# A fused attention and two-layer MLP kernel: two sums of each pair stay in PSUM, and token work, values and first-pair steps are given other places in the order

## The chip, the cores and the metric

The kernel runs on one core of one Trainium2 chip. The metric is the device time of one execution in microseconds, as the median of several runs. The profile shows one execution: TensorE (PE for matmuls, PEld for weight loads), VectorE (DVE), ScalarE (ACT), GpSimd (POOL) and SyncE (SP, which issues the DMAs).

## The reference

Forgetting attention on 4 batches of 8 heads, 576 positions, 64 values a head, then a gated MLP and a second MLP on the 2304 tokens of width 512, all fp32:

```python
cum = np.cumsum(np.maximum(s, 0.0), axis=-1)
bias = -(cum[:, :, :, None] - cum[:, :, None, :])
scores = np.where(causal, -1e9, scale * q @ k.T + np.minimum(bias, 0.0))
attn = softmax(scores)
x = (attn @ v) laid out as [2304, 512]
# first MLP: w_gate, w_val [512, 1536], w_out [1536, 512]
g = x @ w_gate
x = (g * sigmoid(g) * (x @ w_val)) @ w_out
# second MLP: w_in [512, 2048], w_out [2048, 512]
h = x @ w_in
out = (h * sigmoid(h)) @ w_out
```

## The kernel before, in words

Every fp32 product is made of three matmuls on a high and a low part (`mm3`, L448 to L450): high by high, high by low, low by high. Cutting a tile into the two parts is a copy on ScalarE (`copy`, L100) and a subtraction, mostly on GpSimd (L426, L460, L518).

The first layer is a row of 36 chunks of weights, nine for each batch (`L1`: six "gv" chunks for the gate and value matrices, three "o1" chunks for the way down). The attention of batch 0 stands ahead of them. Chunks 0 to 26 run in a loop (`for c in range(last)` in `body`) in which the MLP of batch b is interleaved with the attention of batch b + 1: the table `at` says after which quarter of a chunk the scores, the transposes (L271, L277) and the values (`value`, L312, bank `pv`) of a head pair are issued. In this loop only TensorE's order is that of the code; a scheduler sets the order of the other engines. The weights come packed as 64-bit numbers, and in batch 0 each chunk also unpacks the weights of the next (`unpack`, L369 to L374: two ScalarE and two VectorE steps on each of four pieces; the intermediate `dk` lies in one of the four banks of the pool `ps_m`, which the gates, `pgv`, and the sums of the way down, `po`, use by turns). Unpacked pieces are stored to memory (`w_store`) for the later batches. The list `later` deals 32 pieces of the second layer's weights out over the chunks from batch 1 on; each is loaded a chunk ahead of its unpacking (`ahead_load`, `ahead`).

Chunks 27 to 35 are batch 3, without attention; all engines run in the order of the code. The results of layer 1 are stored to `x_d` (L490) as they are complete. The tokens of the first of three groups are loaded again (`x2_load`, L508), combined (`x2_sub`, L532) and cut (`x2_cut`, L518) for the second layer, in the steps of the lists `more` and `extra`.

The second layer has 24 steps, one for each of three token groups t and eight pairs p of weight columns. In each, `up2` forms four products of 2x2 blocks by seven products xi = 0 to 6 (a scheme like Strassen's and Winograd's) in four banks a, d, b, c of `ps_m`; copies of banks (`s0`, `s1`, `s4`, L621), sums with them (L626, L632, L636), a tanh (L591), the gate product (`gated`, L598) and the cut into `h` follow on the other engines. `down2` of the step before (L657 to L659) then adds into `acc` (L664, L666). Weights of the second layer are combined (`u_sum`), cut (`u_cut`) and, for the later groups, stored (`u_store`, to `wu_d`). The dictionary `fills` says behind which product of `up2` ("u", xi) or which part of `down2` ("d", n) such work is issued. The temporaries of these steps take the place in SBUF of tiles of the first layer.

Of the kernel before, what the change touches and what calls it, by code (L numbers as in the profile page):

```python
# [56 lines left out]
def kernel(  # L57
# [520 lines left out]

    def up2(i, fill):
        t, p = steps[i]  # L580
# [13 lines left out]
        def gated(k):  # L594
            src = u[k]
            if k == 0:
                u[k] = part("u0")
            nc.vector.scalar_tensor_tensor(out=u[k], in0=th[k], scalar=1.0, in1=src, op0=ALU.add, op1=ALU.mult)  # L598
# [6 lines left out]
        for name, k, xi, bank in UP:  # L605
# [22 lines left out]
            if xi == 4:  # L628
                nc.gpsimd.tensor_tensor(out=tmp["s1"], in0=tmp["s1"], in1=tmp["s4"], op=ALU.add)
                nc.gpsimd.tensor_tensor(out=tmp["s1"], in0=tmp["s1"], in1=tmp["u2"], op=ALU.add)  # L630
            if xi == 5:
                nc.vector.tensor_tensor(out=part("c12"), in0=o, in1=tmp["u2"], op=ALU.add)  # L632
                tanh(1, tmp["c12"])
                gated(1)
            if xi == 6:
                nc.vector.tensor_tensor(out=part("c21"), in0=o, in1=tmp["u2"], op=ALU.add)  # L636
                tanh(3, tmp["s1"])
                cut(1)
                gated(3)
                tanh(2, tmp["c21"])  # L640
                cut(3)
                gated(2)
                cut(2)
            for f in fill.get(("u", xi), []):
# [105 lines left out]
    def body():  # L750
# [33 lines left out]
        for i in range(NPR * CW // DW):  # L784
            later[len(L1) + i if i < 18 else 3 * len(L1) + (i - 18) // 2].append(i)
        p2["wt"], p2["st"] = wt_p, raw_p
        for c in range(last):
# [3 lines left out]
            if b + 1 < B:  # L791
                k, u0 = c % len(L1), (b + 1) * H
                if k < H:
                    if k > 1:
                        at[0].append(lambda x=u0 + k - 2: value(x))
                    at[0].append(lambda x=u0 + k: scores(x))
                    if k > 0:
                        at[2].append(lambda x=u0 + k - 1: transpose(x))
                else:
                    at[0] += [lambda x=u0 + k - 2: value(x), lambda x=u0 + k - 1: transpose(x)]  # L800
                    at[2].append(lambda x=u0 + k - 1: value(x))
            for n, stp in enumerate(cur):
# [21 lines left out]
        for c in range(last, n1):  # L824
# [14 lines left out]
            g = nc.gpsimd  # L839
            if k == 2:  # L840
                more[2].append(lambda: x2_load(0))
            if k == 3:
                extra = [
                    lambda: x2_sub(0, 1),
                    lambda: (x2_cut(0, 0, None, g), x2_sub(0, 2)),
                    lambda: x2_cut(0, 1, p2["t", 1], g),
                    lambda: x2_cut(0, 2, None, g),
                ]
            if k == 6:
                extra = [  # L850
                    lambda: (x2_cut(0, 3, p2["t", 2], g), x2_sub(0, 3)),
                    lambda: (x2_cut(0, 4, p2["t", 3], g), x2_sub(0, 4)),
                    lambda: x2_cut(0, 5, None, g),
                    lambda: x2_cut(0, 6, p2["t", 4], g),
                ]
            if k == 7:
# [8 lines left out]
            for n, stp in enumerate(cur):  # L865
                if n == 0:
                    wst.pop(c - 1, None)
                stp()
                todo = more[n] if len(cur) == 4 else more[n // 2] if n % 2 == 0 else extra[n // 2 : n // 2 + 1]
                late, stores = stores, []  # L870
                for f in todo:
                    f()
                if n % (len(cur) // 4) == 0:
                    e = n // (len(cur) // 4) - 2
                    if 0 <= e < len(later[c]):
                        stores.append(later[c][e])
                for i in late:
                    ahead_store(i)
        first_layer.close()
        p2["acc"] = pool("acc2", 1, scope=second_layer)  # L880
        p2["h"] = pool("h2", 8, scope=second_layer)
        p2["tmp"] = pool("tmp2", 1, scope=second_layer)
        p2["wt2"] = pool("wt2", 4, scope=second_layer)
        p2["st"] = pool("st", 4, scope=second_layer)
        fills = [{} for _ in range(len(steps) + 1)]

# [3 lines left out]
        g, v = nc.gpsimd, nc.vector  # L890
        put(0, ("u", 0), lambda: u_cut(0, "D", v), lambda: u_raw(1, "D"))
        put(0, ("u", 3), lambda: u_store(0))
        put(0, ("u", 5), lambda: u_raw(2, "Z"))
        put(0, ("u", 6), lambda: u_store(1, "ZS"))
# [17 lines left out]
        for t in range(1, TG):  # L912
# [3 lines left out]
            put(i - 1, ("d", 7), lambda t=t: x2_cut(t, 0, None, g))  # L916
            put(i, ("u", 0), lambda t=t: x2_cut(t, 1, p2["t", 1], g), lambda t=t: x2_sub(t, 2))
            put(i, ("u", 1), lambda t=t: (x2_sub(t, 3), x2_sub(t, 4)))
            put(i, ("d", 1), lambda t=t: x2_cut(t, 2, None, v))
# [6 lines left out]
        for i in range(len(steps)):  # L926
            up2(i, fills[i])
            if i > 0:
# [50 lines left out]
```

## Time and profile before

| | |
|---|---|
| median of 3 runs | 1092.18 us (1090.01 to 1092.25) |
| the profiled execution | 1095.51 us, its span 1093.7 us |
| TensorE busy | 1038.3 us (95%), 7008 matmuls |
| VectorE, ScalarE, GpSimd busy | 60%, 52%, 56% |
| mean granted clock of TensorE | 0.978 |

Busy time of TensorE near the whole span leaves some 55 us of idle time. Part of the idle time lies in the attention of batch 0, ahead of 97 us, which the change doesn't touch.

### The profile page before, as it was taken

To read this page: it belongs to the slowest core of one execution; us is meant where nothing else is said; L and a number is where in the kernel's file an instruction comes from. 1 tells how busy PE (TensorE), PEld (TensorE's weight loads), DVE (VectorE), ACT (ScalarE), POOL (GpSimd) and SP (SyncE) were. 2 spreads that over 40 slices of the span, in tenths; PEclk is the share of its full clock that TensorE was granted. 3 is DMA by queue.
4 is the path that set the end of the run, shared out by engine and by line. 5 is a ranking of instruction groups with operands and counts; after the bars stand their busy time and mean duration, and the time that the engine had idled before them with its cause. 6 is when DMAs were issued, how large, how long until landed. Compare 5 with 4: busy or idle time off the path is not lost.

```text
span 1093.7 us, 19585 instructions
## 1 busy us (share of the span) xinstructions
PE 1038.3 (95%) x7008; PEld 963.9 (88%) x7008; DVE 654.3 (60%) x1529; ACT 565.1 (52%) x1251; POOL 607.3 (56%) x702
## 2 busy tenths in 40 slices
PE   8779899989999999999999998799989999999998
PEld 5448889879989899898999998799989999999998
DVE  5668676835655546546534657667785454744554
ACT  6658776735665546666424554454443433443331
POOL 4555656554766557757435767466675343743342
PEclk8879999999999999999999999999999999999999
DMA  9556586563546375332335662858767664564521
GB/s 224 140 171 207 195 243 211 164 184 120 179 125 177 110 203 157 115 132 93 122 111 192 238 191 103 301 218 286 278 259 238 231 252 162 181 245 164 183 77 58
DMA packets 70481, 197.96 MB, mean 181 GB/s; under 512 B 9008, under 2 KB 28464, under 8 KB 64240
## 3 DMA queue, kind: packets, MB, share of 16 engines
q1 hardware_dynamic: 70384, 196.72, 55.1%
q8 instruction: 55, 0.90, 0.4%
q14 instruction: 42, 0.34, 0.1%
HBM read 146.28 MB, written 50.41 MB: 180 GB/s over the span
## 4 chain that ended last, share of the span: by engine, by line
PE 72%; DVE 11%; DMA 5%; ACT 5%; issue 3%; POOL 2%; SPq 0%; DVEq 0%; ACTq 0%; POOLq 0%
PE pgv L448 7%; PE pgv L450 7%; PE pgv L449 7%; PE po L657 5%; PE po L659 5%; PE po L658 5%; PE pu L615 4%; PE pu L619 4%; PE pu L618 4%; PE pv L312 4%; PE po L448 4%; PE po L450 4%; PE po L449 4%; PE psc L201 4%; PE ptr L271 3%
## 5 line engine op out<-in xcount | busy, mean ns | idle before, releaser
L448 PE MATMUL pgv<-xt,wt 128*128 128x288 f32 x768 | 230.1, 300 | 6.9 <-DVE acc L488 3.5
L449 PE MATMUL pgv<-xt,wt 128*128 128x288 f32 x768 | 226.3, 295 | 0.0
L450 PE MATMUL pgv<-xt,wt 128*128 128x288 f32 x768 | 226.3, 295 | 0.0
L426 POOL TENSOR_TENSOR wt<-wraw,wt 128x1024 fp32r<-128x1024 f32 x72 | 172.2, 2404 | 94.3 <-ACT wt L100 92.1
L448 PEld LDWEIGHTS pgv<-xt,wt 128*128 128x128 f32 x768 | 144.3, 188 | 19.3 <-issue 7.0
L449 PEld LDWEIGHTS pgv<-xt,wt 128*128 128x128 f32 x768 | 144.3, 188 | 0.0
L450 PEld LDWEIGHTS pgv<-xt,wt 128*128 128x128 f32 x768 | 144.2, 188 | 0.0
L657 PE MATMUL po<-h,wt 128*128 128x384 f32 x384 | 131.7, 343 | 3.0 <-DVE acc L666 2.2
L460 POOL TENSOR_TENSOR h<-u,h 128x288 fp32r<-128x288 f32 x96 | 82.9, 867 | 89.3 <-ACT h L100 89.2
L659 PE MATMUL po<-h,wt 128*128 128x384 f32 x384 | 129.1, 336 | 0.0
L658 PE MATMUL po<-h,wt 128*128 128x384 f32 x384 | 129.0, 336 | 0.0
L615 PE MATMUL pu<-x,wt 128*128 128x384 f32 x336 | 114.8, 342 | 9.7 <-ACT s L621 9.7
L231 ACT ACTIVATE e<-e,m 64x64 f32<-64x64 f32 (+4 forms) x160 | 88.5, 554 | 60.0 <-DVE m L218 59.2
L448 PE MATMUL po<-h,wt 128*128 128x288 f32 x384 | 115.2, 300 | 0.8 <-DVE acc L488 0.6
L619 PE MATMUL pu<-x,wt 128*128 128x384 f32 x336 | 114.5, 341 | 0.0
L618 PE MATMUL pu<-x,wt 128*128 128x384 f32 x336 | 114.3, 340 | 0.0
L450 PE MATMUL po<-h,wt 128*128 128x288 f32 x384 | 113.3, 295 | 0.0
L449 PE MATMUL po<-h,wt 128*128 128x288 f32 x384 | 113.1, 294 | 0.0
L100 ACT ACTIVATE h<-u 128x288 fp32r<-128x288 f32 (+1 forms) x120 | 54.8, 457 | 105.2 <-DVE u L458 82.5
L666 DVE SCALAR_TENSOR_TENSOR acc<-po,acc 128x384 f32<-128x384 f32 x168 | 86.5, 548 | 22.6 <-PE po L659 22.2
L457 DVE SCALAR_TENSOR_TENSOR u<-th,pgv 128x288 f32<-128x288 f32 x96 | 43.2, 450 | 93.9 <-ACT th L455 79.2
L621 ACT ACTIVATE s<-pu 128x384 f32<-128x384 f32 x72 | 35.2, 490 | 110.2 <-PE pu L619 110.2
(99 smaller groups left out, 2345.2 us busy)
## 6 DMA issues: line engine op xcount, KB each, us to landing
wt<-wu_d SPq DMA_DIRECT2D x32, 1024.0 KB, 6.2
wraw<-w SPq DMA_DIRECT2D x54, 512.0 KB, 4.7
r<-in_w_dram SPq DMA_DIRECT2D x52, 512.0 KB, 6.2
wu_d<-wt SPq DMA_DIRECT2D x16, 1024.0 KB, 6.3
wt<-wu_d SPq DMA_DIRECT2D x16, 768.0 KB, 4.6
qkr<-in_qk_dram SPq DMA_DIRECT2D x32, 288.0 KB, 6.9
w<-wraw SPq DMA_DIRECT2D x18, 512.0 KB, 4.2
cumb<-cum_d SPq DMA_DIRECT2D x15, 576.0 KB, 8.4
```

What stands on the lines that cost most here:

```text
L231: nc.scalar.activation(out=e[:r, hd, :wd], in_=e[:r, hd, :wd], func=AF.Exp, bias=m[hd][:r], scale=-1.0, accum_out=l[:r, hd : hd + 1],)
L426: engines[WL[phase[c]][e]].tensor_tensor(out=wl, in0=t, in1=wh.bitcast(F32), op=ALU.subtract)
L448: nc.tensor.matmul(out=ps[:, :n], lhsT=a, rhs=xh, start=(k == 0), stop=False)
L449: nc.tensor.matmul(out=ps[:, :n], lhsT=a, rhs=xl, start=False, stop=False)
L450: nc.tensor.matmul(out=ps[:, :n], lhsT=c, rhs=xh, start=False, stop=(k == last))
L615: nc.tensor.matmul(out=o, lhsT=a, rhs=x[:, 0, kk], start=fresh and kk == 0, stop=False, skip_group_check=True)
L618: nc.tensor.matmul(out=o, lhsT=a, rhs=x[:, 1, kk], stop=False, **more)
L619: nc.tensor.matmul(out=o, lhsT=c, rhs=x[:, 0, kk], stop=kk == 1, **more)
L657: nc.tensor.matmul(out=ps, lhsT=a, rhs=hi, start=f == 0, stop=False)
L658: nc.tensor.matmul(out=ps, lhsT=a, rhs=lo, start=False, stop=False)
L659: nc.tensor.matmul(out=ps, lhsT=c, rhs=hi, start=False, stop=f == 1)
L666: nc.vector.scalar_tensor_tensor(out=a, in0=ps, scalar=0.5, in1=a, op0=ALU.mult, op1=ALU.add)
```

## The change

In the second layer two of the sums of a pair are written back into their banks in place of SBUF, and their gate products read them there into tiles of their own (`w1`, `w2`); `gated(1)` is issued one product later. The closing steps of the first pair (`tail`) are issued behind products 0, 1 and 2 of the second pair. Two loads (`u_raw`) are issued ahead of the first pair. The pool of the temporaries is opened behind those of the weights, so that it lies elsewhere. At the end of a group one cut of tokens is issued in the way down. In batch 3 the load, the subtractions and the cuts of tokens are dealt out over chunks 0 to 6 of the batch; the list `later` starts a chunk later. In the loop over chunks, `value` moves from the start of a chunk to its first quarter, or from the half to three quarters.

```diff
         def gated(k):
             src = u[k]
-            if k == 0:
-                u[k] = part("u0")
+            if k != 3:
+                u[k] = part(f"w{k}")
             nc.vector.scalar_tensor_tensor(out=u[k], in0=th[k], scalar=1.0, in1=src, op0=ALU.add, op1=ALU.mult)
...
             if xi == 4:
-                nc.gpsimd.tensor_tensor(out=tmp["s1"], in0=tmp["s1"], in1=tmp["s4"], op=ALU.add)
-                nc.gpsimd.tensor_tensor(out=tmp["s1"], in0=tmp["s1"], in1=tmp["u2"], op=ALU.add)
+                nc.gpsimd.tensor_tensor(out=part("w3"), in0=tmp["s1"], in1=tmp["s4"], op=ALU.add)
+                nc.gpsimd.tensor_tensor(out=tmp["w3"], in0=tmp["w3"], in1=tmp["u2"], op=ALU.add)
             if xi == 5:
-                nc.vector.tensor_tensor(out=part("c12"), in0=o, in1=tmp["u2"], op=ALU.add)
-                tanh(1, tmp["c12"])
+                nc.vector.tensor_tensor(out=o, in0=o, in1=tmp["u2"], op=ALU.add)
+                tanh(1, o)
+            if xi == 6:
                 gated(1)
-            if xi == 6:
-                nc.vector.tensor_tensor(out=part("c21"), in0=o, in1=tmp["u2"], op=ALU.add)
-                tanh(3, tmp["s1"])
-                cut(1)
-                gated(3)
-                tanh(2, tmp["c21"])
-                cut(3)
-                gated(2)
-                cut(2)
+                nc.vector.tensor_tensor(out=o, in0=o, in1=tmp["u2"], op=ALU.add)
+                tail = [
+                    lambda: (tanh(3, tmp["w3"]), cut(1)),
+                    lambda: (gated(3), tanh(2, o), cut(3), gated(2)),
+                    lambda: cut(2),
+                ]
+                for e, f in enumerate(tail):
+                    if i == 0:
+                        later_on.setdefault(("u", e), []).append(f)
+                    else:
+                        f()
...
-            later[len(L1) + i if i < 18 else 3 * len(L1) + (i - 18) // 2].append(i)
+            later[len(L1) + 1 + i if i < 17 else 3 * len(L1) + (i - 17) // 2].append(i)
...
                     if k > 1:
-                        at[0].append(lambda x=u0 + k - 2: value(x))
+                        at[1].append(lambda x=u0 + k - 2: value(x))
                     at[0].append(lambda x=u0 + k: scores(x))
...
-                    at[0] += [lambda x=u0 + k - 2: value(x), lambda x=u0 + k - 1: transpose(x)]
-                    at[2].append(lambda x=u0 + k - 1: value(x))
+                    at[1] += [lambda x=u0 + k - 2: value(x), lambda x=u0 + k - 1: transpose(x)]
+                    at[3].append(lambda x=u0 + k - 1: value(x))
...
-            if k == 2:
+            if k == 0:
                 more[2].append(lambda: x2_load(0))
-            if k == 3:
-                extra = [
-                    lambda: x2_sub(0, 1),
-                    lambda: (x2_cut(0, 0, None, g), x2_sub(0, 2)),
-                    lambda: x2_cut(0, 1, p2["t", 1], g),
-                    lambda: x2_cut(0, 2, None, g),
-                ]
-            if k == 6:
-                extra = [
-                    lambda: (x2_cut(0, 3, p2["t", 2], g), x2_sub(0, 3)),
-                    lambda: (x2_cut(0, 4, p2["t", 3], g), x2_sub(0, 4)),
-                    lambda: x2_cut(0, 5, None, g),
-                    lambda: x2_cut(0, 6, p2["t", 4], g),
-                ]
+            sub = {1: 1, 2: 2, 4: 3, 5: 4}.get(k)
+            cuts = {1: [0], 2: [1], 3: [2, 3], 4: [4], 5: [5], 6: [6]}.get(k, [])
+            if sub:
+                more[0].append(lambda: x2_sub(0, sub))
+            for e, x in enumerate(cuts):
+                src = None if x in (0, 2, 5) else {1: 1, 3: 2, 4: 3, 6: 4}[x]
+                f = lambda x=x, src=src: x2_cut(0, x, None if src is None else p2["t", src], g)
+                if len(cur) == 4:
+                    more[2].append(f)
+                else:
+                    extra.append(f)
...
-                todo = more[n] if len(cur) == 4 else more[n // 2] if n % 2 == 0 else extra[n // 2 : n // 2 + 1]
+                todo = more[n] if len(cur) == 4 else more[n // 2] if n % 2 == 0 else extra[n // 4 : n // 4 + n // 2 % 2]
...
-        p2["tmp"] = pool("tmp2", 1, scope=second_layer)
         p2["wt2"] = pool("wt2", 4, scope=second_layer)
         p2["st"] = pool("st", 4, scope=second_layer)
-        fills = [{} for _ in range(len(steps) + 1)]
+        p2["tmp"] = pool("tmp2", 1, scope=second_layer)
+        u_raw(1, "D")
+        u_raw(2, "Z")
+        fills, tails = [{} for _ in range(len(steps) + 1)], {}
...
-        put(0, ("u", 0), lambda: u_cut(0, "D", v), lambda: u_raw(1, "D"))
+        put(0, ("u", 0), lambda: u_cut(0, "D", v))
         put(0, ("u", 3), lambda: u_store(0))
-        put(0, ("u", 5), lambda: u_raw(2, "Z"))
...
-            put(i, ("u", 0), lambda t=t: x2_cut(t, 1, p2["t", 1], g), lambda t=t: x2_sub(t, 2))
-            put(i, ("u", 1), lambda t=t: (x2_sub(t, 3), x2_sub(t, 4)))
+            put(i, ("u", 0), lambda t=t: (x2_sub(t, 2), x2_sub(t, 3)))
+            put(i, ("u", 1), lambda t=t: x2_sub(t, 4))
+            put(i, ("d", 0), lambda t=t: x2_cut(t, 1, p2["t", 1], g))
...
-            up2(i, fills[i])
+            up2(i, fills[i], tails if i == 0 else None)
+            fills[i + 1] = {k: tails.pop(k, []) + fills[i + 1].get(k, []) for k in {*tails, *fills[i + 1]}}
```

At the start of chunk 2 TensorE's order before is this: the last gate matmul of chunk 1, the values of a head pair (`pv`), the scores of another (`psc`), the first gate matmul of chunk 2.

```order
L450 MATMUL pgv<-xt,wt 128x288
L312 MATMUL pv<-pt,vz 64x320 x2
L312 MATMUL pv<-pt,vrb 64x256 x2
L312 MATMUL pv<-pt,vrb 64x128 x2
L201 MATMUL psc<-qkr 128x64 x2
L201 MATMUL psc<-qkr 128x192 x2
L201 MATMUL psc<-qkr 128x320 x2
L448 MATMUL pgv<-xt,wt 128x288
```

With the change it is:

```order
L450 MATMUL pgv<-xt,wt 128x288
L201 MATMUL psc<-qkr 128x64 x2
L201 MATMUL psc<-qkr 128x192 x2
L201 MATMUL psc<-qkr 128x320 x2
L448 MATMUL pgv<-xt,wt 128x288
```

The rows of `pv` now stand behind the first gate step of the chunk; the first bank of `ps_m` in chunk 2 is that of a gate.

In chunk 8, the last of batch 0, ScalarE's order before has the unpacking of a second-layer piece (`dk<-r`) ahead of a tanh of the gates (`th<-pgv`); `pt<-ptr` copies transposed scores, `xt<-pv` values.

```order
L100 ACTIVATE pt<-ptr 128x2x384
L370 ACTIVATE dk<-r_3189 128x512
L455 ACTIVATE th<-pgv 128x288
L100 ACTIVATE h<-u 128x288
L455 ACTIVATE th<-pgv 128x288
L100 ACTIVATE wt<-wraw 128x1024 x2
L100 ACTIVATE h<-u 128x288
L100 ACTIVATE xt<-pv 128x320
L100 ACTIVATE pt<-ptr 128x1024
L100 ACTIVATE xt<-pv 128x256
```

With the change it is:

```order
L100 ACTIVATE pt<-ptr 128x2x384
L455 ACTIVATE th<-pgv 128x288
L100 ACTIVATE h<-u 128x288
L455 ACTIVATE th<-pgv 128x288
L100 ACTIVATE wt<-wraw 128x1024 x2
L100 ACTIVATE h<-u 128x288
L100 ACTIVATE xt<-pv 128x320
L100 ACTIVATE pt<-ptr 128x1024
L370 ACTIVATE dk<-r_3366 128x512
L100 ACTIVATE xt<-pv 128x256
```

`dk<-r` has moved behind every tanh of the chunk, with one copy of values behind it.

Between the first and the second pair of the second layer, ScalarE's order before is this, from the copy of product 4 of the first pair on (`s_9230` and `s_9244` are those of products 0 and 1 of the second pair; `c` are the two sums).

```order
L621 ACTIVATE s_9180<-pu 128x384
L591 ACTIVATE th<-c_9190 128x384
L591 ACTIVATE th<-s_9147 128x384
L100 ACTIVATE h_9123<-c_9190 128x384
L591 ACTIVATE th<-c_9203 128x384
L100 ACTIVATE h_9125<-s_9147 128x384
L100 ACTIVATE h_9124<-c_9203 128x384
L621 ACTIVATE s_9230<-pu 128x384
L621 ACTIVATE s_9244<-pu 128x384
L100 ACTIVATE wt<-stage 128x1024
```

With the change it is this (`s_9218` and `s_9236` are now those of the second pair):

```order
L621 ACTIVATE s_9182<-pu 128x384
L591 ACTIVATE th<-pu 128x384
L621 ACTIVATE s_9218<-pu 128x384
L591 ACTIVATE th<-w_9184 128x384
L100 ACTIVATE h_9127<-w_9202 128x384
L621 ACTIVATE s_9236<-pu 128x384
L591 ACTIVATE th<-pu 128x384
L100 ACTIVATE h_9129<-w_9184 128x384
L100 ACTIVATE wt<-stage 128x1024
L100 ACTIVATE wt<-stage 128x768
L591 ACTIVATE th<-pu 128x384
L100 ACTIVATE h_9128<-w_9243 128x384
```

The two copies of the second pair have moved ahead of most closing steps of the first, and a last cut of the first pair (`h_9128`) stands behind the first tanh of the second.

## Rows read from the trace of the kernel before

**Rows 1.** First line of the page.
```profile
span 1093.7 us, 19585 instructions
```

**Rows 2.** Waits of TensorE, 97.7 to 255.6 us: total, times, longest.
```profile
PE pv L312 <- DVE wraw L374: 5.4, 5, 3.1
PE pv L312 <- DVE u L457: 4.9, 1, 4.9
PE pgv L448 <- DVE wraw L374: 1.1, 1, 1.1
...
```

**Rows 3.** Waits of TensorE, 566.1 to 689.5 us (batch 3).
```profile
PE pgv L448 <- DVE acc L488: 3.5, 2, 2.5
PE pgv L448 <- DVE u L457: 2.4, 3, 1.6
PE po L448 <- DVE acc L488: 0.6, 1, 0.6
```

**Rows 4.** Waits of TensorE, 689.5 us to the end (second layer).
```profile
PE pu L615 <- ACT s L621: 9.7, 4, 3.9
PE po L657 <- DVE acc L666: 2.2, 7, 0.4
PE po L657 <- ACT acc L664: 0.9, 2, 0.4
```

**Rows 5.** Windows: busy us (instructions) of PE, PEld, DVE, ACT, POOL; PEclk; DMA.
```profile
236.05:239.46 3.41, 3.41 (x19) 2.40 (x16) 1.12 (x3) 3.17 (x6) 2.21 (x2) 0.50 0.00 0
239.46:242.87 3.41, 3.41 (x29) 3.41 (x28) 2.17 (x3) 1.15 (x2) 3.41 (x3) 1.00 0.37 120
710.50:713.91 3.41, 3.40 (x11) 3.40 (x12) 2.00 (x3) 1.00 (x3) 2.82 (x3) 0.50 0.97 394
713.91:717.32 3.41, 3.41 (x21) 3.41 (x20) 1.62 (x2) 2.70 (x8) 2.88 (x3) 1.00 0.48 194
...
812.90:816.31 3.41, 3.41 (x12) 3.41 (x11) 2.19 (x3) 1.18 (x4) 2.32 (x3) 0.50 0.00 0
```

**Rows 6.** Timeline of ScalarE, chunks 3 and 8: start, duration, [idle before, releaser].
```profile
149.30 1.23 ACT L369 ACTIVATE wraw<-r 128x512 f32<-128x512 f32 x2 [2.56 <-DMA w<-wraw]
...
234.18 0.66 ACT L370 ACTIVATE dk<-r 128x512 uint32<-128x512 uint32 x1 [9.24 <-DMA r<-in_w_dram]
```

**Rows 7.** Timeline of VectorE in batch 3.
```profile
619.26 2.33 DVE L371 SCALAR_TENSOR_TENSOR dk<-z,dk 128x512 uint32<-128x512 uint32 x1
...
623.78 0.68 DVE L371 SCALAR_TENSOR_TENSOR dk<-z,dk 128x512 uint32<-128x512 uint32 x1
```

**Rows 8.** Timeline of SyncE, TensorE and VectorE around the second pair.
```profile
691.30 2.99 SPq L575 DMA_DIRECT2D wu_d<-wt  x3
694.39 1.22 SPq L550 DMA_DIRECT2D stage<-w  x1
...
702.10 0.44 PE L615 MATMUL pu<-x,wt 128*128 128x384 f32 x1 [2.88 <-ACT s L621]
...
704.74 3.18 DVE L561 TENSOR_TENSOR stage<-stage 128x256 f32<-128x256 f32 x4 [3.63 <-DMA stage<-w]
```

**Rows 9.** Groups by line and form: count, busy us, mean ns, idle before.
```profile
L598 DVE SCALAR_TENSOR_TENSOR c<-th,c 128x384 f32<-128x384 f32 x48 | 49.6, 1034 | 20.7 <-ACT th L591 20.7
L598 DVE SCALAR_TENSOR_TENSOR s<-th,s 128x384 f32<-128x384 f32 x24 | 13.4, 558 | 6.4 <-ACT th L591 6.4
L598 DVE SCALAR_TENSOR_TENSOR u<-th,pu 128x384 f32<-128x384 f32 x24 | 13.3, 552 | 63.3 <-ACT th L591 63.3
```

**Rows 10.** Timeline of VectorE, GpSimd and TensorE at the first group's end.
```profile
806.62 0.94 DVE L532 TENSOR_TENSOR stage<-x2r,stage 128x768 f32<-128x768 f32 x1
807.19 2.07 POOL L518 TENSOR_TENSOR x<-stage,x 128x768 fp32r<-128x768 f32 x1 [1.77 <-ACT x L100]
807.49 2.59 DVE L532 TENSOR_TENSOR stage<-x2r 128x768 f32<-128x768 f32 x1
...
812.40 0.44 PE L615 MATMUL pu<-x,wt 128*128 128x384 f32 x1 [2.67 <-ACT s L621]
```

More of the change, by code (lines that the diff above doesn't have):

```diff
@@ L577, in u_store, with up2 @@
             )
-    def up2(i, fill):
+    def up2(i, fill, later_on):
         t, p = steps[i]
```

## The prediction, made before the changed kernel ran

> **What bounds the kernel now.** The first line of the page gives the span, 1093.7 us [rows 1]. I read the waits of TensorE next, stage by stage, because the kernel can only get shorter where TensorE stands idle or runs at the low clock; its other work is the same set of matmuls after the change. In the chunk loop of batch 0 three rows are 11.4 us of idle time [rows 2]; batch 3 has 6.5 us [rows 3]; the second layer 12.8 us [rows 4]. [...] Nearly all of it is TensorE waiting for a bank of PSUM that VectorE or ScalarE has still to empty, so the question at each place is what these engines do instead, and for what they wait.
>
> **Chunk loop of batch 0.** Two things happen. First, the values start a quarter chunk later, behind the scores and the first gate step. The five waits of 5.4 us in all [rows 2] are for banks that held `dk` in the unpacking of the next weights; the order shows that the bank is now wanted by the gate behind the scores, so the scores are the cover, about as long as what stood ahead before. But the order also shows score work of VectorE put between two `dk`, so `dk` is done later; and the unpacking is a chain through memory: ScalarE stood 2.56 us until a store of decoded weights had left its buffer [rows 6], and that store is no earlier now. Of the 6.5 us of the `wraw` rows I count 1.2 as won. From below, each of the six chunks 2 to 7 could lose 0.7 us (4 us in all, a quarter of the 2.56 us wait in each); from above all 6.5 are won. I take a value near the lower end because the chain's waits are the longest that these rows show.
>
> Second, chunk 8. There the 4.9 us wait comes from one ScalarE row: `dk<-r` stood 9.24 us for a load and held back the tanh behind it [rows 6]. After the change this row stands behind all four tanh of the chunk, and the load is one of the next chunk's, so nothing that TensorE needs is queued behind it but one copy of values. This wins 4.9 us and the clock behind it, 1.2 us [rows 5]. Chunk loop: 1.2 + 4.9 + 1.2 = **7.3 us** (6.1 - 4 = 2.1, to 6.1 + 6.5 = 12.6).
>
> **Batch 3.** The waits are for VectorE (the sums into `acc`, the gate products) [rows 3], in the two chunks where x2 work is bunched. While GpSimd cuts tokens, VectorE's `dk<-z` takes 2.33 us; the next one, alone, 0.68 us [rows 7]: 1.65 us more for each row. Bunched, two unpackings and two subtractions follow one another there, 6.6 us late; spread over six chunks, half as many, 3.3 us, and the four banks that TensorE fills by turns cover most of that. The new order adds a wait: the first load of x2 goes out only half a chunk ahead of its first subtraction, behind which the gate products of that chunk are queued. I take a microsecond or two there as covered by the banks too. I count 4.9 of 6.5 us as won: the second cut of chunk 3 stands at its end, so that chunk 4 has two of them on GpSimd beside two of weights, which leaves about 1 us, and the last piece in chunk 7 about 0.6. Bounds: 3.5, if each chunk with a cut keeps half a microsecond (six chunks, 3 us), and 6.5.
>
> [...]
>
> **First pair into second pair.** Two waits for `s`. The first, 2.88 us [rows 8], is `s` of the second pair in ScalarE's queue behind the closing steps of the first; the order shows that these now stand between the `s` of the second pair. The second, 3.9 us [rows 4], is a chain: the load of `stage` was issued at 694.39 behind three stores that took 2.99 us; VectorE waited 3.63 us for it, until 704.74, then took 3.18 us for the sum, and the products and copies stood behind [rows 8]. Both loads now go out ahead of these stores, so the data lands 3 us earlier or more: VectorE's wait falls to 0.6 us or nothing. What is late next is the half-chain of the first pair: its last product must be out of its bank before the second pair takes it for its product 4, and `s1`, `gated` and three tanh stand in one queue. I leave one wait of 2 us there, and 1.1 us for the first step down, whose cover shrinks. Of 2.9 + 3.9 and the clock of 1.6, 8.4 in all, 8.4 - 2.0 - 1.1 = **5.3 us** is won (3.4, if one wait of 3.4 us stays and the clock falls once; 8.4). The temporaries now lie where the last outputs of layer 1 lay and wait for their stores; the stores are issued well ahead of the first use, so I count nothing. If that cover is gone, the wait for `s` comes back in full, which is the lower bound.
>
> **Closing steps of every pair.** `gated` of the two sums took 1034 ns in place in SBUF; the same operation on a bank takes 552, the third one, on `s` in SBUF, 558 [rows 9]. So it isn't the place of the operand alone: what stretches the 1034 is GpSimd beside it. I take 552, which is the row with the same operands as now. Two products a pair are 2 x 0.48 = 1.0 us earlier on the chain that ends in the last `h` of a pair; `gated(1)` also moves behind product 6, off the queue ahead of the last sum. The waits at the first step down are 2.2 + 0.9 us in nine places, 0.43 at most [rows 4], all shorter than 1.0. The cost is that two banks are held longer; the eight steps of down behind cover that. **2.7 us** (1.5, if the held banks bring half of it back; 3.1).
>
> **Group ends.** One wait of 2.67 us. VectorE's subtraction beside GpSimd's cut took 2.59 us, and 0.94 the one ahead of it [rows 10]. The cut moves to the next down step, so 2.59 - 0.94 = 1.6 us go, the wait falls to about 1.0, and the clock should hold, 1.5 us: **3.1 us** (1.0, if the clock falls all the same; 4.4).
>
> **The sum.** 7.3 + 4.9 + 5.3 + 2.7 + 3.1 = 23.3 us. The profiled execution took 1095.51 us (its span and 1.8 us around it): 1072.2. The median of the three runs, 1092.18, is 3.3 us under it; taken off, 1068.9, said as **1069 us**. The five lower bounds make 2.1 + 3.5 + 3.4 + 1.5 + 1.0 = 11.5, so 1080.7; the upper ones 35.0, so 1057.2.
>
> **Rivals.**
> *The waits move.* [...] Chance 0.20.
>
> *Everything goes.* All waits of [rows 2 to 4] and the clock: the upper bound, 1057. For it: each of these waits has a cover in the new order but those of `wraw`. Against: the order of VectorE above. 0.12.
>
> *The bank is dearer.* `gated` from a bank could be held up as much as the 1034 ns row, when GpSimd is not the cause; then the closing steps win nothing: 1072. Against: 552 and 558 [rows 9]. 0.05. [...]
>
> *The change doesn't do what it says*, as the scheduler of ScalarE and VectorE puts the moved work back where it waits: within 0.2% of 1092. The order speaks against it. 0.05.
>
> *Slower.* One mechanism: in chunks 2 to 7 the unpacking of the next weights is later than the scores cover, since VectorE does score work between two `dk`; each chunk then ends at store, landing and ScalarE's `wraw<-r`. The other terms make 22 us, so it decides from 22/6 = 3.7 us for each of six chunks; at the price of twice the 2.56 us wait, 5.1 us each, the time is 1092.2 - 22.1 + 30.7 = 1101. For it: the chain's wait in [rows 6]. Against: VectorE is not full there. 0.04.
>
> **How the numbers follow.** The forecast (1064 to 1076) has 0.54. **1060 to 1082** leaves out half of the second rival (0.06), the two last (0.09) and a quarter of the first (0.05), 0.20 in all. About 0.2%, 2.2 us, is what a measurement of this kernel can tell from no change. Faster: 0.54 + 0.20 + 0.12 + 0.05 = 0.91; 0.01 of the first rival reaches further up, which leaves 0.90; same 0.05; slower 0.05.
>
> **What would show it.** Right: no ScalarE row with a load of 9 us in chunk 8 and no half clock at 236; waits in batch 3 of 1.6 us in all; VectorE's sum of the third step without a wait for `stage`; `gated` on banks at 0.55 us and no wait at the first step down; at most one half-clock stretch after 256 us. Wrong: rows `pgv<-wraw` of several microseconds in chunks 2 to 7; waits of `pu` for a tail product; a wait of VectorE for `x2r` in batch 3.

## The result, and the profile after

The changed kernel takes 1073.3 us (median of 4 runs, 1072.31 to 1076.13) against 1092.22 (1090.01 to 1092.34): the ratio is 0.9836, with a 95% interval of 0.9813 to 0.9858. That is 18.9 us; the forecast was 23.2 (1069), its range 1060 to 1082. The profiled execution of after took 1073.3 us, 22.2 less than that of before.

The first line of the page and TensorE's waits in the three stretches that [rows 1 to 4] show of before: total, times, longest.

```profile
span 1071.5 us, 19575 instructions
...
PE pgv L448 <- DVE wraw L374: 3.1, 2, 2.0
PE po L448 <- DVE xt L327: 1.7, 1, 1.7
PE ptr L277 <- DVE rl L240: 0.5, 1, 0.5
...
PE po L448 <- DVE u L457: 3.1, 2, 1.5
PE pgv L448 <- DVE u L457: 1.6, 3, 0.6
PE po L448 <- DVE acc L488: 0.6, 1, 0.6
...
PE po L660 <- DVE acc L669: 4.0, 2, 2.3
PE pu L615 <- ACT s L621: 1.9, 2, 1.1
PE po L660 <- ACT acc L667: 1.7, 1, 1.7
```

The wait of 4.9 us in chunk 8 and most of those for `s` are gone. But idle rows don't say where 22 us went, so I cut both executions at the same matmuls (first product of a chunk or step) and read the windows between. A row is start and end, length, then busy us (instructions) of PE, PEld, DVE, ACT, POOL, granted clock, DMA. Before: the prologue, chunks 0 to 8, batches 1 and 2, batch 3, the first two steps, steps 2 to 6, the first group's end, steps 9 to 14, the second group's end, the rest.

```profile
0.00:84.64 84.64, 64.61 (x384) 41.74 (x384) 53.98 (x213) 53.08 (x143) 42.36 (x108) 0.80 0.66 176
84.64:256.90 172.26, 159.49 (x1206) 144.75 (x1205) 111.18 (x307) 112.22 (x256) 94.81 (x131) 0.98 0.65 197
256.90:566.14 309.24, 309.24 (x2398) 282.82 (x2397) 176.06 (x527) 174.94 (x422) 190.69 (x248) 1.00 0.46 140
566.14:689.50 123.36, 116.93 (x867) 114.81 (x865) 70.24 (x103) 59.21 (x110) 78.81 (x49) 1.00 0.52 172
689.50:721.56 32.06, 25.27 (x134) 24.55 (x133) 19.10 (x25) 18.77 (x36) 18.93 (x15) 0.95 0.73 279
721.56:803.21 81.65, 80.18 (x452) 78.58 (x451) 62.10 (x98) 40.48 (x72) 52.79 (x41) 1.00 0.80 286
803.21:839.41 36.20, 33.53 (x181) 32.92 (x181) 26.98 (x39) 14.80 (x28) 23.68 (x17) 0.95 0.54 197
839.41:935.81 96.40, 95.97 (x541) 94.23 (x541) 48.46 (x83) 36.08 (x75) 39.68 (x37) 1.00 0.62 224
935.81:969.35 33.54, 32.59 (x181) 31.35 (x181) 24.25 (x36) 14.81 (x28) 21.29 (x16) 1.00 0.43 141
969.35:1093.73 124.38, 120.46 (x679) 118.12 (x678) 61.91 (x106) 40.67 (x85) 44.22 (x42) 1.00 0.41 151
```

The same ten windows after:

```profile
0.00:82.01 82.01, 61.38 (x385) 39.57 (x385) 53.99 (x213) 53.09 (x143) 42.45 (x108) 0.83 0.67 182
82.01:245.75 163.74, 158.55 (x1206) 143.60 (x1204) 108.09 (x307) 110.95 (x256) 94.97 (x131) 0.99 0.68 207
245.75:557.35 311.60, 311.60 (x2399) 283.27 (x2397) 180.40 (x525) 173.25 (x420) 193.74 (x248) 1.00 0.44 137
557.35:679.49 122.14, 116.75 (x867) 114.80 (x865) 70.54 (x105) 60.30 (x112) 77.33 (x49) 1.00 0.56 180
679.49:706.09 26.60, 23.82 (x134) 23.01 (x133) 14.57 (x25) 18.23 (x36) 18.79 (x15) 1.00 0.89 335
706.09:784.79 78.70, 78.70 (x451) 78.70 (x451) 56.19 (x98) 40.18 (x72) 51.55 (x41) 1.00 0.82 296
784.79:821.43 36.64, 33.61 (x181) 32.96 (x181) 24.50 (x39) 14.77 (x28) 22.51 (x17) 0.95 0.55 203
821.43:915.87 94.44, 94.44 (x541) 94.44 (x541) 43.69 (x83) 35.68 (x75) 37.63 (x37) 1.00 0.62 227
915.87:949.37 33.50, 31.79 (x182) 31.47 (x182) 22.25 (x36) 14.89 (x28) 20.59 (x16) 1.00 0.44 146
949.37:1071.52 122.15, 118.66 (x679) 118.34 (x678) 56.27 (x106) 40.19 (x85) 41.80 (x42) 1.00 0.41 152
```

The lengths, before less after, against the terms of the prediction:

| stage | forecast | measured |
|---|---|---|
| prologue, not touched | 0 | 2.6 |
| chunks 0 to 8 | 7.3 | 8.5 |
| batches 1 and 2 | 0 | -2.4 |
| batch 3 | 4.9 | 1.2 |
| first two steps | 5.3 | 5.5 |
| closing steps, all other steps | 2.7 | 7.1 (2.95 + 1.96 + 2.23) |
| group ends | 3.1 | -0.4 (-0.44 + 0.04) |
| sum | 23.3 | 22.2 |

The reader is to see that the sum came out nearly right from four terms that were off, three one way and one the other, and from 2.6 us of the prologue, which is the same code: without it the stages are 19.6 us shorter, not 22.2. Batches 1 and 2 have TensorE busy without a gap both times and still differ by 2.4 us; so do steps 9 to 14 by 2.0, of which before shows only 0.4 as idle (96.40 - 95.97).

### The profile page after: what moved, and what is told of

Read it like the earlier page. It is cut to its first block, busy times and chain, and to the rows that moved or that the text cites. A ratio compares the mean times of both kernels' runs of the same rounds, so it can differ in the third digit from the quotient of the medians.

```text
span 1071.5 us, 19575 instructions
## 1 busy us (share of the span) xinstructions
PE 1029.3 (96%) x7008; PEld 960.2 (90%) x7008; DVE 630.5 (59%) x1529; ACT 561.5 (52%) x1251; POOL 601.4 (56%) x702
## 4 chain that ended last, share of the span: by engine, by line
PE 81%; DVE 8%; ACT 4%; issue 3%; POOL 2%; DMA 2%; DVEq 0%; POOLq 0%; ACTq 0%; SPq 0%
PE pgv L448 8%; PE pgv L450 8%; PE pgv L449 8%; PE po L660 6%; PE po L662 6%; PE po L661 6%; PE pu L615 5%; PE pu L619 5%; PE pu L618 5%; PE po L448 5%; PE pv L312 4%; PE po L449 4%; PE po L450 4%; PE psc L201 3%; PE ptr L271 3%
## 5 line engine op out<-in xcount | busy, mean ns | idle before, releaser
L603 POOL TENSOR_TENSOR h<-w,h 128x384 fp32r<-128x384 f32 x96 | 96.0, 1023 | 158.8 <-ACT h L100 158.8
L598 DVE SCALAR_TENSOR_TENSOR w<-th,pu 128x384 f32<-128x384 f32 x72 | 39.9, 554 | 87.0 <-ACT th L591 87.0
```

The lines of the kernel that those rows point to most:

```text
L603: nc.gpsimd.tensor_tensor(out=lo, in0=u[k], in1=hi.bitcast(F32), op=ALU.subtract)
```

## Experiments

Each is the changed kernel with one thing different, unless said otherwise; stage lengths are between the same matmuls as above, from its profiled execution. The prologue, which all share, was 82.0 to 84.6 us long, so stages tell more than the times do. Where a stage has the code of the change, chunks 0 to 8 took 163.1 to 164.7 us, batch 3 122.0 to 122.2 (120.66 in experiment 2, see 9) and the first two steps 26.6; smaller differences say nothing. In the diffs, `...` stands for lines that are left out.

**1. Values back at the start of a chunk** (in all batches).

```diff
-                        at[1].append(lambda x=u0 + k - 2: value(x))
+                        at[0].append(lambda x=u0 + k - 2: value(x))
...
-                    at[1] += [lambda x=u0 + k - 2: value(x), lambda x=u0 + k - 1: transpose(x)]
-                    at[3].append(lambda x=u0 + k - 1: value(x))
+                    at[0] += [lambda x=u0 + k - 2: value(x), lambda x=u0 + k - 1: transpose(x)]
+                    at[2].append(lambda x=u0 + k - 1: value(x))
```

> The change with the values back at the start of a chunk, in all batches. A, the term of the prediction: the later values win 1.2 us in batch 0 and nothing in batches 1 and 2, so the time is 1074.5 us and batches 1 and 2 (start of chunk 9 to start of chunk 27) stay at 311.6 us. B, each group of value matmuls that stands alone between gates costs TensorE two more switches between kinds of matmul, 0.15 us for each of 16 groups: batches 1 and 2 go back to 309.2 us, 2.4 us less; chunks 0 to 8 lose what the waits for the unpacked weights cost, 2 to 4 us, less 1.2 us of switches; 1072 to 1074 us.

1073.65 us (ratio 0.9837, 0.9812 to 0.9862). Chunks 0 to 8 take 166.28 us, 2.5 more than with the change; batches 1 and 2 309.24, 2.4 less. B is right on both, and the two cancel. The diff shows that one transpose of each batch moves along with the values, in the change as here.

**2. Values later only in batch 0.**

```diff
-                        at[1].append(lambda x=u0 + k - 2: value(x))
+                        at[b == 0].append(lambda x=u0 + k - 2: value(x))
...
```

> The change with the values later only while batch 0 runs, and at the start of a chunk in batches 1 and 2. A: as the change, 1073.3 us, since batches 1 and 2 have no idle time to win or lose. B: 309.2 us in place of 311.6 for chunks 9 to 26, so 1070.9 us.

1071.36 us (0.982, 0.9794 to 0.9846); batches 1 and 2 take 309.25 us as B said. What the later values cost there is seen in TensorE's timeline of after, where a value group stands between gates:

```profile
279.01 0.30 PE L448 MATMUL pgv<-xt,wt 128*128 128x288 f32 x1
279.14 0.29 PE L449 MATMUL pgv<-xt,wt 128*128 128x288 f32 x1
279.27 0.29 PE L450 MATMUL pgv<-xt,wt 128*128 128x288 f32 x1
279.49 0.76 PE L312 MATMUL pv<-pt,vz 128*64 128x320 f32 x4
280.08 0.82 PE L312 MATMUL pv<-pt,vrb 128*64 128x256 f32 x8
280.83 0.40 PE L448 MATMUL pgv<-xt,wt 128*128 128x288 f32 x1
281.07 0.29 PE L449 MATMUL pgv<-xt,wt 128*128 128x288 f32 x1
```

Gate matmuls start 0.13 us apart; into the group it is 0.22, and the first one behind it is followed after 0.24: 0.09 + 0.11 = 0.20 us more. Ahead of the scores, as before, the values shared these switches with them. That was so for 12 of the 16 groups of batches 1 and 2; the other four, in the last chunk of each attention, have the same company in both kernels, transposes or none. 2.36 us over 12 groups is 0.20 us a group, not the 0.15 over 16 of the expectation, and no idle row shows it.

**3. The two sums in SBUF again**, the first gate product behind product 5.

```diff
-                nc.vector.tensor_tensor(out=o, in0=o, in1=tmp["u2"], op=ALU.add)
-                tanh(1, o)
+                nc.vector.tensor_tensor(out=part("c12"), in0=o, in1=tmp["u2"], op=ALU.add)
+                tanh(1, tmp["c12"])
+                gated(1)
...
```

> The change with the two sums of each pair in SBUF again and the first gate product behind product 5. A, the term of the prediction, from idle rows: 2.7 us, so 1076.0 us. B, a wait of TensorE that is shorter than the tail of the matmul before it shows no idle time and still moves every later start: from the starts of the products of steps 2 to 23 the change won 0.6 us in each step of the first group and 0.26 us in each of the others, 7 us in all, so 1080.4 us, with the fifth product of each way down starting 0.24 us or more late.

1086.47 us (0.9954, 0.9937 to 0.9971), worse than both said. Steps 2 to 6, 9 to 14 and the rest take 81.36, 96.40 and 124.72 us, 7.2 more than with the change: there B is right. The first two steps take 30.34 us, 3.7 more, and the group ends 1.9 more, which neither theory had. The sums in the banks, together with the later place of one gate product, are worth 12.8 us beside the second layer's 392.0.

How a wait costs more than its idle row is seen in TensorE's timeline of before, at the fifth product of a way down:

```profile
834.67 0.33 PE L658 MATMUL po<-h,wt 128*128 128x384 f32 x1
834.84 0.34 PE L659 MATMUL po<-h,wt 128*128 128x384 f32 x1
835.14 0.44 PE L657 MATMUL po<-h,wt 128*128 128x384 f32 x1
835.42 0.34 PE L658 MATMUL po<-h,wt 128*128 128x384 f32 x1
```

Matmuls start 0.17 us apart and are 0.33 us long (the profile models their ends), so they overlap. L657 starts 0.30 us after the one ahead, and the next 0.28 us after it: 0.24 us lost with no idle time at all. In after, from the second way down on, all starts at the same place are 0.17 or 0.18 us apart. Where an idle row says 0.43 us, the same starts lie 0.7 us later.

**4. Pieces of the second layer from chunk 9 on, as before.**

```diff
-            later[len(L1) + 1 + i if i < 17 else 3 * len(L1) + (i - 17) // 2].append(i)
+            later[len(L1) + i if i < 18 else 3 * len(L1) + (i - 18) // 2].append(i)
```

> The change with the pieces of the second layer dealt out from chunk 9 on, as before. A: the row of ScalarE that waits for its load stands ahead of a tanh in chunk 8 again, and with it the wait of 4.9 us and the half clock of 1.2 us: 1079.4 us. B: with the values no longer at the start of the chunk the four banks of the gates cover part of it, so 1 to 3 us more, 1074 to 1076 us.

1082.83 us (0.9917, 0.9894 to 0.994). Chunks 0 to 8 take 170.54 us, 6.8 more. ScalarE's timeline of this kernel has the row back:

```profile
232.50 0.66 ACT L370 ACTIVATE dk<-r 128x512 uint32<-128x512 uint32 x1 [8.49 <-DMA r<-in_w_dram]
233.06 0.43 ACT L100 ACTIVATE h<-u 128x288 fp32r<-128x288 f32 x1
```

It now holds back a copy of `h`, and TensorE waits 4.1 us for it. A is right about the stage, and 0.7 us short; the time is 3.4 us over A's, as the prologue of this execution, 84.49 us, is 2.5 us longer too.

**5. Token work of batch 3 bunched again.**

```diff
+            if k == 2:
+                more[2].append(lambda: x2_load(0))
+            if k == 3:
+                extra = [
+                    lambda: x2_sub(0, 1),
...
```

> The change with the token work of batch 3 bunched in chunks 3 and 6 again; all else, the later list of pieces too, as the change. A, the term of the prediction: the spreading wins 4.9 us, so batch 3 (start of chunk 27 to start of the second layer) takes 127 us in place of 122.1 and the time is 1078 us. B, the spreading only moves the places where VectorE's unpacking runs into a cut on GpSimd: batch 3 takes 123.4 us, as in the kernel before, and the time is 1074.5 us.

1077.24 us (0.9854, 0.9825 to 0.9883; runs 1075.08 to 1078.38). Batch 3 takes 123.49 us, 1.4 more, as B said of the stage. The window of batch 3 here is to be read against that of after:

```profile
559.60:683.09 123.49, 118.22 (x867) 116.33 (x866) 71.84 (x105) 60.27 (x112) 79.49 (x49) 0.99 0.56 178
```

TensorE is idle for 5.3 us here and for 5.4 with the change. The 1.4 us is busy time at the low clock: for 3.41 us, right behind a wait of 2.48 us for `acc`, the granted clock is 0.50. The kernel before has that wait too, at 664.32 us, without a half clock behind it. So the spreading isn't shown to win any of the waits. The rest of the difference of the medians, 2.6 us, lies outside the stage: the prologue of this execution is 2.2 us longer than that of after.

**6. The old order at the group ends.**

```diff
-            put(i, ("u", 0), lambda t=t: (x2_sub(t, 2), x2_sub(t, 3)))
-            put(i, ("u", 1), lambda t=t: x2_sub(t, 4))
-            put(i, ("d", 0), lambda t=t: x2_cut(t, 1, p2["t", 1], g))
+            put(i, ("u", 0), lambda t=t: x2_cut(t, 1, p2["t", 1], g), lambda t=t: x2_sub(t, 2))
+            put(i, ("u", 1), lambda t=t: (x2_sub(t, 3), x2_sub(t, 4)))
```

> The change with the token work at the group ends in the old order. A, the term of the prediction: 3.1 us more, 1076.4 us, with a wait of 2.7 us for an s of the last step of the first group. B, by the step starts the new order won nothing (the wait moved from an s to the fifth product of the way down): 1073.3 us within 0.7.

1073.0 us (0.9816, 0.979 to 0.9843), as B said. The two group ends take 34.97 and 32.82 us, 1.7 and 0.7 less than with the change. The new order loses; most of the 1.7 us is a half clock (see the last section).

**7. Closing steps of the first pair at once.**

```diff
-                    if i == 0:
+                    if later_on is not None:
...
-            up2(i, fills[i], tails if i == 0 else None)
+            up2(i, fills[i], None)
```

> The change with the closing steps of the first pair issued at once, not inside the second pair. A: the first wait of the transition, 2.9 us for an s, comes back, since ScalarE's queue is as before: 1076 us. B: with the sums in the banks the closing steps are shorter by 1 us, and the load for the third step is early, so at most 1.5 us come back: 1073.3 to 1074.8 us.

1074.88 us (0.9831, 0.9801 to 0.9862). The first two steps take 26.65 us against 26.60, so nothing comes back and A is wrong. Deferring the closing steps is worth nothing beside the rest of the change.

**8. The two loads inside the first pair again**, the temporaries' pool ahead of the weights' pools.

```diff
+        p2["tmp"] = pool("tmp2", 1, scope=second_layer)
         p2["wt2"] = pool("wt2", 4, scope=second_layer)
         p2["st"] = pool("st", 4, scope=second_layer)
-        p2["tmp"] = pool("tmp2", 1, scope=second_layer)
-        u_raw(1, "D")
-        u_raw(2, "Z")
...
-        put(0, ("u", 0), lambda: u_cut(0, "D", v))
+        put(0, ("u", 0), lambda: u_cut(0, "D", v), lambda: u_raw(1, "D"))
         put(0, ("u", 3), lambda: u_store(0))
+        put(0, ("u", 5), lambda: u_raw(2, "Z"))
```

> The change with the two loads of weights issued inside the first pair again and the temporaries' pool ahead of the weights' pools. A: the wait of 3.9 us behind VectorE's wait for the load comes back, and the half clock of 1.6 us with it, 1078.5 us. B: with the closing steps deferred, the sum that waits for the load stands between other work and hides part of it, 2 us more, 1075.3 us.

1079.7 us (0.9878, 0.9855 to 0.99). The first two steps take 33.95 us, 7.3 more, longer even than before the change. VectorE's timeline here:

```profile
687.65 0.56 DVE L636 TENSOR_TENSOR pu<-pu,u 128x384 f32<-128x384 f32 x1
695.70 1.55 DVE L561 TENSOR_TENSOR stage<-stage 128x256 f32<-128x256 f32 x4 [7.49 <-DMA stage<-w]
697.17 0.55 DVE L598 SCALAR_TENSOR_TENSOR w<-th,w 128x384 f32<-128x384 f32 x1
```

In the change the same sum waits for nothing: it starts at 688.22 us, as the row ahead of it ends. A is right about the wait and 1.9 us short of its price: two gate products of the deferred closing steps are queued behind the sum, and TensorE waits 6.9 us for one of them. That the place of the pool has a part in it wasn't tried apart.

**9. Cuts of batch 3 on VectorE.**

```diff
-                f = lambda x=x, src=src: x2_cut(0, x, None if src is None else p2["t", src], g)
+                f = lambda x=x, src=src: x2_cut(0, x, None if src is None else p2["t", src])
```

> The change with the cuts of tokens of batch 3 on VectorE in place of GpSimd, at the same places. A, VectorE's unpacking is late only because it waits for a cut on GpSimd that started first: the seven cuts become rows of about 1.25 us on VectorE, the unpacking rows go to 0.69 us, and most of the waits of batch 3 (5.3 us of idle time and 0.3 us each that no idle row shows) go: batch 3 takes 117 to 118 us in place of 122.1, the time is 1069 us. B, VectorE is full there, and more work makes it later: batch 3 takes 122 us or more, 1073 to 1076 us.

1071.26 us (0.9798, 0.9777 to 0.9818). Batch 3 takes 118.66 us, 3.5 less, nearly what A said. In batch 3 `dk` is a tile in SBUF (pool `dec_p`) and not in a bank, so VectorE's unpacking rows have two SBUF inputs. In the change, VectorE, GpSimd and TensorE stand so at one place, in what chunk 29 issues to the first two:

```profile
599.30 1.95 POOL L518 TENSOR_TENSOR x<-tt,x 128x768 fp32r<-128x768 f32 x1 [0.29 <-ACT x L100]
...
599.59 2.20 DVE L374 SCALAR_TENSOR_TENSOR z<-r,dk 128x512 uint32<-128x512 uint32 x1
...
602.21 0.40 PE L448 MATMUL po<-h,wt 128*128 128x288 f32 x1 [1.54 <-DVE u L457]
```

In experiment 2, where the cut came 0.3 us later, the same instructions of GpSimd and VectorE stand so:

```profile
599.62 2.39 POOL L518 TENSOR_TENSOR x<-tt,x 128x768 fp32r<-128x768 f32 x1 [0.58 <-ACT x L100]
...
599.62 0.69 DVE L374 SCALAR_TENSOR_TENSOR z<-r,dk 128x512 uint32<-128x512 uint32 x1
```

Where GpSimd is first by 0.29 us, VectorE's row ends 0.54 us behind GpSimd's (601.79, 601.25); where it isn't, VectorE takes 0.69 us, the wait of 1.54 us that TensorE has there in the change is gone, and batch 3, whose code is that of the change, takes 120.66 us, 1.5 less. So where GpSimd's row starts first, VectorE's is the longer (2.20 us against 0.69), and where it doesn't, GpSimd's (2.39 against 1.95). With the cut on VectorE, the three rows take 0.73, 0.69 and 0.95 us.

**10. VectorE's first cut of a group's end in the way up.**

```diff
-            put(i, ("d", 1), lambda t=t: x2_cut(t, 2, None, v))
+            put(i, ("u", 5), lambda t=t: x2_cut(t, 2, None, v))
```

> The change with VectorE's first cut at a group's end issued behind product 5 of the way up, not in the way down beside GpSimd's cuts. A, the wait at the fifth product of the way down (2.3 and 1.7 us, 0.28 us more each that no idle row shows, and a half clock of 1.3 us behind the first) comes from this cut, which takes 2.6 us beside GpSimd's: step 7 to step 9 takes 33 us in place of 36.6, step 15 to 17 31.7 in place of 33.5, the time is 1068.5 us. B, in the way up the cut and its copy stand ahead of the closing steps, and the wait moves to an s or to the last products: within 1 us of 1073.3.

1070.93 us (0.979, 0.977 to 0.981). The group ends take 33.10 and 32.42 us, 3.5 and 1.1 less, as A said. The wait that goes is at the seventh product of the way down, not at the fifth as the expectations have it: 36 matmuls of that way down stand ahead of it, six a product. In the change, VectorE's cut stood beside four of GpSimd's in a row, and the row that empties the bank stood behind it:

```profile
798.77 8.65 POOL L518 TENSOR_TENSOR x<-stage,x 128x768 fp32r<-128x768 f32 x4
...
798.79 2.63 DVE L518 TENSOR_TENSOR x<-x2r,x 128x768 fp32r<-128x768 f32 x1 [1.13 <-ACT x L100]
801.35 1.01 DVE L669 SCALAR_TENSOR_TENSOR acc<-po,acc 128x384 f32<-128x384 f32 x2
...
801.95 0.45 PE L660 MATMUL po<-h,wt 128*128 128x384 f32 x1 [2.27 <-DVE acc L669]
```

In the way up the cut takes 1.00 us, and in place of the waits of 2.3 and 1.7 us there are two of 0.9 us together.

**11. Experiments 2, 9 and 6 together.**

> The change with three things together: values later only in batch 0, cuts of tokens of batch 3 on VectorE, the old order at the group ends. If the parts add up as the stages showed them apart: 1073.3 - 2.4 (batches 1 and 2) - 4.5 (batch 3) - 2.3 (group ends) = 1064.1 us. If VectorE is full in batch 3: 1068.6 us or more.

1067.41 us (0.9763, 0.9744 to 0.9783). The stages do what they did apart (309.25, 118.55, 34.96, 32.79 us: 2.4, 3.6, 1.7 and 0.7 less than with the change), 8.4 us in all, so VectorE isn't full in batch 3; the medians differ by 5.9. Of the 2.5 us between, 2.1 lie in the prologue (84.14 us here, 82.01 there), the rest in the spread of runs.

**12. Experiments 2, 9 and 10 together.**

> The change with the values later only in batch 0, the cuts of tokens of batch 3 on VectorE, and VectorE's first cut of a group's end behind product 5. If the stages add up: the kernel with the old order at the group ends had 35.0 us from step 7 to step 9 and 32.8 from 15 to 17; with the cut in the way up 33.1 and 32.4 were seen, so 2.3 us less than its 1067.4: 1065.1 us. If the two pieces of token work disturb each other, no better than 1067.4 us.

1064.38 us (0.972, 0.9705 to 0.9735), against 1094.6 for the kernel before on the same chip: the best version, and what the stages add up to (1065.1). Batches 1 and 2 take 309.25 us, batch 3 118.56, the group ends 33.05 and 32.42.

## Why the prediction was right, and where its steps were wrong

**Base.** The sum was 23.3 us, the two profiled executions differ by 22.2, of which 2.6 lie in the prologue: there the granted clock is 0.83 in place of 0.80, in work that the change doesn't touch. It is after that stands apart here, not before: its prologue of 82.01 us is the shortest of all fourteen traces, and before's 84.64 us is like most (83.9 us or more in eleven of the twelve experiments). The change itself is worth 19.6 us, and the medians say 18.9, against 23.3 in the sum. That the time came so near the forecast is partly luck: batches 1 and 2, batch 3 and the group ends fell short by 2.4, 3.7 and 3.5 us, and the closing steps won 4.4 us more than forecast. The terms for the clock, 1.2, 1.6 and 1.5 us, were estimates from the counts of matmuls in the windows of [rows 5] (21 in 816.31 to 819.72 us for the third). No run shows the first two by themselves; the granted clock of their stages went from 0.98 to 0.99 and from 0.95 to 1.00. The half clock at the first group's end is left, and costs 1.6 us beside experiment 9 (last section).

**Chunk 8: right.** 6.1 us were forecast; undoing it costs 6.8 (experiment 4).

**Values later: right in batch 0, a cost missed behind it.** The term was 1.2 us; in batch 0 the move wins 2.5 (experiment 1). The step that failed is that TensorE's "other work is the same set of matmuls after the change": the set is the same, but each of the 12 groups of values that now stand alone costs 0.20 us more, 2.4 us in batches 1 and 2, where nothing waited (experiment 2).

**Batch 3: wrong, 1.2 for 4.9 us.** The step that failed is that VectorE, spread, is late "half as many" times, 3.3 us, and "the four banks that TensorE fills by turns cover most of that". Of VectorE's unpacking rows and token subtractions in batch 3, eight take over 2 us in before, eight in experiment 5 and eight with the change, where seven of them stand behind a token cut on GpSimd and one behind a cut of weights: a spread cut holds back VectorE as long as a bunched one (rows of 2.20 to 2.48 us with the change, 2.18 to 2.97 in before) if it starts just ahead of an unpacking row, and the new places are those of the unpacking. Of the waits 5.3 us are left, for 1.6 forecast. Experiment 5 shows the same: undoing the spreading brings back no wait (5.3 us idle against 5.4), only a half clock that costs 1.4 us. Experiment 9 shows the cause by taking the cut off GpSimd, which makes batch 3 3.5 us shorter. Against before about a microsecond of waits is gone; undoing the list `later`, which deals its pieces differently in batch 3 too, brings no more than 0.3 us of it back (experiment 4, 122.45 us), and the rest stays open.

**First two steps: right in size, 5.5 for 5.3 us, but one part does nothing.** The loads' place carries it (experiment 8, 7.3 us when undone), and the sums in the banks are needed too (3.7, experiment 3); the two overlap, as both are more than 5.5 together. Deferring the closing steps, which the prediction gave the first wait of 2.88 us, is worth no more than 0.05 us (experiment 7).

**Closing steps: the mechanism right, the size 7.1 for 2.7 us.** The gate products on banks take 554 ns in the mean, as this group of after shows (all three of a pair that read a bank), and the waits at the fifth product of the way down are gone from the second way down on, as forecast.

```profile
L598 DVE SCALAR_TENSOR_TENSOR w<-th,pu 128x384 f32<-128x384 f32 x72 | 39.9, 554 | 87.0 <-ACT th L591 87.0
```

The cause that the prediction gave for the 1034 ns, GpSimd beside it, is borne out by the traces. In before each of the 48 products on sums in SBUF starts while a row of GpSimd runs and ends 0.41 or 0.42 us behind it, as here:

```profile
895.06 1.01 POOL L630 TENSOR_TENSOR s<-s,u 128x384 f32<-128x384 f32 x1
...
895.61 0.88 DVE L598 SCALAR_TENSOR_TENSOR c<-th,c 128x384 f32<-128x384 f32 x1 [0.59 <-ACT th L591]
```

With the change 54 of the 72 products on banks start beside a row of GpSimd too, and take 555 ns. The mis-sized part is the price of a wait, taken from [rows 4] as idle time in nine places, 3.1 us at most. From the third step on nearly every step of before started its fifth product late, with or without an idle row: 0.24 us where there was none, 0.57 to 0.7 us where the row says 0.3 to 0.4.

**Group ends: wrong, -0.4 for 3.1 us.** The wait for `s` did shrink, 2.67 to 0.8 us. The step that failed is that the cut "moves to the next down step" at no price: there it stands in a row of four on GpSimd, VectorE's own cut is held back to 2.6 us, and the bank of the seventh product is emptied late. So the wait moved, to a place that the prediction doesn't name. The half clock too stayed (0.95 in that window); without it, as in experiment 9 (35.08 us), the first group's end would have won 1.1 us.

**Rivals.** "The waits move" came true for batch 3 (5.3 us left) and the group ends (waits of 2.3 and 1.7 us at the seventh product), not for chunks 2 to 7 nor the second pair (26.60 us for 32.06). The dearer bank did not: 554 ns. "Everything goes" did not: 18 us of waits are left in the three stretches. The slower case did not: there are two waits for `wraw` of 3.1 us in all.

## What to carry to other kernels

Price a wait by the starts of the instructions around it, not by idle time: where instructions overlap, a wait can show no gap and still cost 0.24 us in step after step, as in the way down here. When work on GpSimd is spread or moved, look which VectorE instruction with two SBUF inputs starts just behind it at each new place (here such rows took 2.2 us for 0.69); if that one is on the path, putting the work on VectorE itself can be cheaper (here 3.5 us in batch 3). Move a small group of matmuls out of its company only in the stage where a wait pays for it (here 2.5 us won in batch 0, 2.4 lost in batches 1 and 2).

## What the runs showed of the hardware that was not expected

- A group of value matmuls alone between gates costs 0.20 us beyond its own work: 0.09 us ahead of its first matmul and 0.11 us behind the first gate after it.
- The clock doesn't follow from a wait's length alone. At the first group's end the same wait of 2.3 us stood in the change and in experiment 9; the granted clock of the window was 0.95 in the one and 1.00 in the other, and the stage 36.64 and 35.08 us long. So 1.6 us of the 3.5 that experiment 10 won there, and most of the 1.7 of experiment 6, is this clock. In six other experiments that stage has the code of the change; in all of them it took 36.6 to 36.9 us at 0.95, so experiment 9 is the exception.
- The prologue, the same code in all kernels, was 82.0 to 84.6 us long, and its mean clock 0.83 to 0.80 in the two that are shown. Differences of 2 us between medians of four runs are of that size, and say little by themselves.
